# Who prepares the expert weights of a fused attention, MLP and mixture-of-experts kernel: VectorE with GpSimd, or VectorE alone

## The chip, the core and the metric

The kernel runs on one core of a Trainium2 chip. The metric is the device time of one execution in microseconds (us). The engines of the core run side by side, each through its own list of instructions in order: TensorE (PE in the profile, with PEld for its weight loads), VectorE (DVE), ScalarE (ACT), GpSimd (POOL) and SyncE (SP), which here issues the transfers between the memory on the chip and HBM. They wait for each other through semaphores.

## What is computed

The reference does three things in a row, in float32: attention over keys and values that are averaged in groups of eight, a two-layer MLP, and a mixture of eight experts. Only the last one matters here:

```python
def _moe2_ref(x, w_gate, w1, w2):          # x 2304 x 512, w1 8 x 512 x 1024, w2 8 x 1024 x 512
    logits = x @ w_gate
    ...                                     # exp and eight Sinkhorn steps give P, 2304 x 8
    for e in range(E):
        h = np.maximum(x @ w1[e], 0.0)
        ye = h @ w2[e]
        out += P[:, e:e + 1] * ye
```

## The kernel before, in words

**Numbers in two parts.** A product of two float32 matrices is made from three products of a faster format (fp32r): each matrix is split into a high part, which ScalarE rounds off, and a low part, which is the difference between the matrix and its high part. `halves` (line 964) does this: `activate` for the high part (`whi`, `vhi`, `gh`), then one `tensor_tensor` subtraction for the low part (`wlo`, `vlo`, `gl`), recorded at line 557 inside the helper `tt`.

**Seven products in the place of eight.** Each matrix is cut in four blocks, and sums and differences of the blocks (Strassen's scheme in Winograd's form, products P1 to P7) are multiplied.

**Units and steps.** The experts' weights come in 16 units, u = 0 to 15, each of 512 of the 1024 hidden columns of an expert. The tokens come in three pairs of blocks, taken in the order 1, 0, 2. So there are 48 steps (lines 1595 and 1630); a unit's weights serve three steps running. In a step the first layer (`first_layer`, line 1158, TensorE at line 1178, banks `px`, `py`, `pv`) of one step is interleaved with the second layer (`strassen_layer`, line 1555, TensorE at line 1565, banks `pc`, `qc`) of the step before it.

**The weights of a unit.** `w1_pieces` (line 1358) and `w2_pieces` (line 1394) load a unit's raw blocks (`raw`) and then make seven pieces each. Each function has four `combine` steps, which add or subtract two raw blocks into one of them (128 x 512, `raw<-raw` or `raw<-raw,raw` in the profile), and seven `cut` steps, which split a block (`whi` and `wlo`, or `vhi` and `vlo`). That is 22 `tensor_tensor` instructions of 128 x 512 a unit. The buffers for the pieces hold just one unit (W1 and W2 are 14 tiles, line 454), so a piece of the next unit can be written only when the last step of the present unit has read its own.

**Who waits for VectorE and ScalarE in a step.** In the first layer, `py<-px` (line 1184) is ScalarE's copy of one bank into another before TensorE goes on in it, and `pv<-py,s` (line 1189) is VectorE's sum of a bank and a copy, after which TensorE may use the bank `py` again. `c`, `spare`, `sf`, `gh`, `gl` make the next layer's operands, and `acc` gathers the results (line 1550).

**The order is planned.** No engine's order is written by hand: `Graph` (line 153) holds every step as a node with its engine and an estimated time, gives each a due time from its successors back (`latest`, line 208; a node that may run on two engines is counted with the longer of its two times), and then lists the nodes in simulated time (`schedule`, line 273): on each engine it takes, among the nodes that could start within a fraction of a microsecond of the earliest, the one that is due first. Nodes with `port=True` and GpSimd's nodes are not put side by side in the plan. Where a node may run on VectorE or GpSimd, the planner chooses:

```python
ALONE = [True]

def VG(n):
    return V(n) if ALONE[0] else {"engine": ("V", "G"), "us": (two(n), pool(n)), "port": True}
```

The `combine` and `cut` steps of the weights take their engine from `VG(FU)` (lines 1378, 1414 and, through `halves`, 968), with FU = 512. Before, `ALONE[0]` is set in one place only, at line 1235, to whether the task there is one of the first four; when the steps of the experts are recorded it is False.

Of the kernel before, what the change touches and what calls it, by code (L numbers as in the profile page):

```python
# [438 lines left out]
ALONE = [True]  # L439
# [9 lines left out]
def fused_kernel(ctx: ExitStack, tc: tile.TileContext, qT, kT, kS, vS, v0, k1, v1, wa1, wb1, wa2, wb2, wg, out):  # L449
# [908 lines left out]
    def w1_pieces(u):  # L1358

        src, w = [], {}  # L1360
        for i in range(2):
            src.append(buf(k_raw, [P, 2, FU], F32, "raw"))
        for i, t in enumerate(src):
            load(lambda t=t: t.tile, lambda i=i: wa2[u, :, i], P * 2 * FU * 4,
                 writes=[(t, 0), (t, 1)] + [(src[1], "room")] * (i == 0))

        def a(i, j):
            t = src[i - 1]
            return (t, j - 1), lambda: t[:, j - 1, :]

        def cut(name, what):
            parts = piece_tiles((k_w1, k_w1), ("whi", "wlo"), [P, FU])
            halves(FU, what[1], what[0], lambda k: parts[k].tile, parts)
            for h in range(2):
                w[name, h] = parts, lambda h=h: [t[:, h * HD:(h + 1) * HD] for t in parts]

        def combine(out, x, y, op):
            tt(VG(FU), out[1], x[1], y[1], op, [b[0] for b in (x, y) if b[0] != out[0]], [out[0]])

        a11, a12, a21, a22 = a(1, 1), a(1, 2), a(2, 1), a(2, 2)  # L1380
        cut("P1", a11)
        cut("P4", a22)
        combine(a22, a21, a22, ALU.add)
        cut("P5", a22)
        combine(a21, a11, a21, ALU.subtract)
        combine(a22, a22, a11, ALU.subtract)
        cut("P6", a22)
        cut("P2", a12)
        cut("P7", a21)
        combine(a12, a12, a22, ALU.subtract)  # L1390
        cut("P3", a12)
        return w

    def w2_pieces(u, goal=FAR):

        src, w = [], {}
        for h in range(2):
            t = buf(k_raw, [P, 2, DM], F32, "raw2")
            src.append(t)
        for h, t in enumerate(src):  # L1400
            load(lambda t=t: t.tile, lambda h=h: wb2[u, :, h], P * 2 * DM * 4,
                 writes=[(t, 0), (t, 1)] + [(src[1], "room")] * (h == 0))

        def b(h, d):
            t = src[h - 1]
            return (t, d - 1), lambda: t[:, :, (d - 1) * HD:d * HD]

        def cut(name, what):
            w[name] = parts = piece_tiles((k_w2, k_w2), ("vhi", "vlo"), [P, FU])
            halves(FU, what[1], what[0], lambda k: parts[k].tile.rearrange("p (g n) -> p g n", g=2), parts,  # L1410
                   goal=goal)

        def combine(out, x, y):
            tt(VG(FU), out[1], x[1], y[1], ALU.subtract, [q[0] for q in (x, y) if q[0] != out[0]], [out[0]])

        b11, b12, b21, b22 = b(1, 1), b(1, 2), b(2, 1), b(2, 2)
        cut("P1", b11)
        combine(b11, b12, b11)
        cut("P5", b11)
        combine(b12, b22, b12)  # L1420
        combine(b11, b22, b11)
        cut("P6", b11)
        cut("P2", b21)
        cut("P7", b12)
        cut("P3", b22)
        combine(b21, b21, b11)
        cut("P4", b21)
        return w
# [37 lines left out]
    def x_loaded(pair):  # L1466

        x = {}
        for name in ORDER:
            t = buf(k_x, [P, 2, 2, NB], F32R, "xc")  # L1470
            load(lambda t=t: t.tile.bitcast(F32), lambda name=name: xc[pair, ORDER.index(name)], P * 4 * NB * 4,
                 reads=[kept_x[pair, name]], writes=[t])
            x[name] = [t], lambda t=t: (t[:, 0], t[:, 1])
        return x
# [153 lines left out]
    boxes = [{} for _ in range(NTP)]  # L1628
    g.lap = False
    for n, (u, pair) in enumerate(steps):  # L1630
        if pair == steps[0][1]:
            w1, w2 = w1_pieces(u), w2_pieces(u, FAR if u else end - 40.0)
        pieces = {}
        first_layer(w1, ready if n == 0 else x_loaded(pair), strassen_result(pieces), goals1[n])
        own = {2: (b_x, b_y)} if n == len(steps) - 1 else None
        strassen_layer(pair, u, pieces, w2, boxes[pair], goals2[n], own)
# [60 lines left out]
```

## Time and profile before

| | us |
|---|---|
| median of 3 runs | 1916.88 |
| lowest and highest | 1916.5 and 1919.01 |
| the profiled execution's own time | 1917.53 |
| its span, from first to last instruction | 1915.8 |
| TensorE busy | 1891.6 |
| VectorE busy | 1511.9 |
| ScalarE busy | 1098.1 |
| GpSimd busy | 360.3 |

The span lies 1.73 us under the profiled execution's own time, and that execution lies 0.65 us over the median. Busy time adds the durations of an engine's instructions. TensorE's granted clock is at its upper level, 2.4 GHz, through the span. The experts' steps begin at about 500 us; a unit takes 87.9 us, and 16 of them reach to the end.

### The profile page before, as it was taken

To read this page: it belongs to the slowest core of one execution; us is meant where nothing else is said; L and a number is where in the kernel's file an instruction comes from. 1 tells how busy PE (TensorE), PEld (TensorE's weight loads), DVE (VectorE), ACT (ScalarE), POOL (GpSimd) and SP (SyncE) were. 2 spreads that over 40 slices of the span, in tenths; PEclk is the share of its full clock that TensorE was granted. 3 is DMA by queue.
4 is the path that set the end of the run, shared out by engine and by line. 5 is a ranking of instruction groups with operands and counts; after the bars stand their busy time and mean duration, and the time that the engine had idled before them with its cause. 6 is when DMAs were issued, how large, how long until landed. Compare 5 with 4: busy or idle time off the path is not lost.

```text
span 1915.8 us, 33914 instructions
## 1 busy us (share of the span) xinstructions
PE 1891.6 (99%) x13032; PEld 1850.2 (97%) x13032; DVE 1511.9 (79%) x2720; ACT 1098.1 (57%) x2372; POOL 360.3 (19%) x264
## 2 busy tenths in 40 slices
PE   9999999999999999999999999999999999999999
PEld 7799998899999999999999999999999999999999
DVE  7998856987687777777787787777777877878776
ACT  5875435675566665555556555565555555555653
POOL 0203332252112121212112021212121120212120
PEclk9999999999999999999999999999999999999999
DMA  8856662577665646546546455565465464655553
GB/s 265 245 197 234 237 164 80 196 265 256 232 234 223 239 175 242 223 176 234 217 174 264 168 234 226 191 238 214 179 240 210 181 264 157 245 215 195 234 203 127
DMA packets 104762, 406.76 MB, mean 212 GB/s; under 512 B 11160, under 2 KB 15896, under 8 KB 102552
## 3 DMA queue, kind: packets, MB, share of 16 engines
q1 hardware_dynamic: 102616, 400.01, 56.1%
q0 software_dynamic: 1984, 4.59, 1.4%
q8 instruction: 102, 1.67, 0.4%
q14 instruction: 60, 0.49, 0.1%
HBM read 363.40 MB, written 41.16 MB: 211 GB/s over the span
## 4 chain that ended last, share of the span: by engine, by line
PE 85%; DVE 9%; issue 2%; DMA 2%; ACT 2%; SPq 0%; POOL 0%; POOLq 0%; DVEq 0%; ACTq 0%
PE pc L1565 18%; PE py L1178 15%; PE qc L1565 15%; PE pv L1178 10%; PE px L1178 10%; PE po L989 3%; PE po L991 3%; PE po L990 3%; PE ph L989 2%; PE ph L991 2%; PE ph L990 2%; DVE sf L557 2%; DVE raw L557 1%; DVE gl L557 1%; DVE vlo L557 1%
## 5 line engine op out<-in xcount | busy, mean ns | idle before, releaser
L1565 PE MATMUL pc<-vhi,gl 128*128 128x256 f32 x1152 | 318.2, 276 | 0.0
L1565 PE MATMUL pc<-vlo,gh 128*128 128x256 f32 x1152 | 318.0, 276 | 0.0
L1565 PE MATMUL pc<-vhi,gh 128*128 128x256 f32 x1152 | 318.0, 276 | 0.0
L1178 PE MATMUL py<-xc,whi 128*128 128x384 f32 x1152 | 297.1, 338 | 9.4 <-ACT py L540 5.1
L1565 PE MATMUL qc<-vhi,gh 128*128 128x256 f32 x864 | 238.7, 276 | 0.2 <-DVE qc L557 0.2
L1565 PE MATMUL qc<-vlo,gh 128*128 128x256 f32 x864 | 238.5, 276 | 0.0
L1565 PE MATMUL qc<-vhi,gl 128*128 128x256 f32 x864 | 238.5, 276 | 0.0
L540 ACT ACTIVATE gh<-sf 128x384 fp32r<-128x384 f32 x384 | 195.4, 524 | 63.6 <-DVE sf L557 59.2
L557 DVE TENSOR_TENSOR gl<-sf,gh 128x384 fp32r<-128x384 f32 x384 | 204.0, 561 | 31.8 <-ACT gh L540 31.6
L557 POOL TENSOR_TENSOR raw<-raw 128x512 f32<-128x512 f32 x47 | 62.3, 1326 | 874.3 <-DVE wlo L557 492.2
L1565 PEld LDWEIGHTS pc<-vhi,gl 128*128 128x128 f32 x1152 | 216.2, 188 | 0.1
L1565 PEld LDWEIGHTS pc<-vhi,gh 128*128 128x128 f32 x1152 | 216.2, 188 | 0.1
L1565 PEld LDWEIGHTS pc<-vlo,gh 128*128 128x128 f32 x1152 | 216.2, 188 | 0.0
L1178 PEld LDWEIGHTS py<-xc,whi 128*128 128x128 f32 x1152 | 199.0, 188 | 17.7 <-ACT py L540 10.3
L1178 PE MATMUL px<-xc,whi 128*128 128x384 f32 x768 | 196.4, 336 | 0.2 <-DMA xc<-xc 0.2
L1178 PE MATMUL pv<-xc,whi 128*128 128x384 f32 x768 | 195.9, 336 | 0.0
L1178 PE MATMUL py<-xc,wlo 128*128 128x384 f32 x576 | 192.6, 334 | 0.0
L1565 PEld LDWEIGHTS qc<-vhi,gh 128*128 128x128 f32 x864 | 162.2, 188 | 0.5 <-DVE qc L557 0.5
L1565 PEld LDWEIGHTS qc<-vhi,gl 128*128 128x128 f32 x864 | 162.2, 188 | 0.0
L1565 PEld LDWEIGHTS qc<-vlo,gh 128*128 128x128 f32 x864 | 162.0, 187 | 0.0
L1178 PEld LDWEIGHTS pv<-xc,whi 128*128 128x128 f32 x768 | 132.1, 188 | 0.0
L540 ACT ACTIVATE qc<-pc 128x256 f32<-128x256 f32 x144 | 53.1, 369 | 136.7 <-PE pc L1565 136.6
(245 smaller groups left out, 4671.4 us busy)
## 6 DMA issues: line engine op xcount, KB each, us to landing
xc<-xc SPq DMA_DIRECT2D x357, 768.0 KB, 6.8
wc<-wac SPq DMA_DIRECT2D x112, 256.0 KB, 4.7
raw<-wb SPq DMA_DIRECT2D x32, 512.0 KB, 7.7
raw<-wa SPq DMA_DIRECT2D x32, 512.0 KB, 3.8
raw<-wa SPq DMA_DIRECT2D x8, 1024.0 KB, 7.3
raw<-wb SPq DMA_DIRECT2D x8, 1024.0 KB, 6.0
wac<-m SPq DMA_DIRECT2D x12, 512.0 KB, 6.3
wac<-cw SPq DMA_DIRECT2D x12, 512.0 KB, 3.1
```

The costliest lines, as they stand in the source:

```text
L540: lambda: nc.scalar.activation(out=out(), in_=in_(), func=func, **{k: v() if callable(v) else v for k, v in more.items()}),
L557: (nc.gpsimd if e == "G" else nc.vector).tensor_tensor(out=out(), in0=in0(), in1=in1(), op=op)
L989: nc.tensor.matmul(out=ps, lhsT=lh, rhs=rh, start=(i == 0), stop=False)
L990: nc.tensor.matmul(out=ps, lhsT=lh, rhs=rl, start=False, stop=False)
L991: nc.tensor.matmul(out=ps, lhsT=ll, rhs=rh, start=False, stop=(i == total - 1))
L1178: nc.tensor.matmul(out=ps(), lhsT=l[:, k], rhs=r[:, c, :], start=(start and c + n == 0), stop=(c + n == 3), skip_group_check=True)
L1565: nc.tensor.matmul(out=ps, lhsT=l[:, r], rhs=m[:, k], start=(start and h + n == 0), stop=(h + n == 3), skip_group_check=True)
```

## The change

One line is added. As the steps of the experts are recorded, `ALONE[0]` is set to whether the unit is not the first, so from the second unit (u = 1) on `VG` gives the planner VectorE alone for the 22 `combine` and `cut` instructions of a unit. Unit 0, and all that is recorded before the experts, keep the choice between the two engines.

```diff
     boxes = [{} for _ in range(NTP)]
     g.lap = False
     for n, (u, pair) in enumerate(steps):
+        ALONE[0] = u > 0
         if pair == steps[0][1]:
             w1, w2 = w1_pieces(u), w2_pieces(u, FAR if u else end - 40.0)
         pieces = {}
```

## Rows read from the trace of the kernel before

**Rows 1.** Busy time by stretches; columns in the first line, x counts instructions.
```profile
core 0: us, PE busy (x) PEld busy (x) DVE busy (x) ACT busy (x) POOL busy (x), PEclk, DMA share, GB/s
0.00:500.00 500.00, 489.76 (x2909) 459.26 (x2910) 404.31 (x668) 292.49 (x584) 126.37 (x93) 1.00 0.64 211
600.00:690.00 90.00, 90.00 (x653) 89.82 (x653) 68.85 (x127) 63.43 (x137) 16.47 (x12) 1.00 0.57 218
690.00:1880.00 1190.00, 1180.23 (x8516) 1172.21 (x8515) 933.19 (x1690) 665.22 (x1490) 201.05 (x149) 1.00 0.56 213
```

**Rows 2.** TensorE's waits, 700 to 1900 us: total, times, longest.
```profile
PE py L1178 <- ACT py L540: 5.1, 13, 0.4
PE py L1178 <- DVE pv L557: 4.4, 14, 0.6
```

**Rows 3.** Timeline of TensorE: start, duration, instruction, idle time before it and releaser.
```profile
1036.32 0.51 PE L1178 MATMUL py<-xc,whi 128*128 128x384 f32 x2
...
1048.94 0.62 PE L1178 MATMUL py<-xc,whi 128*128 128x384 f32 x2 [0.39 <-ACT py L540]
...
1054.31 0.45 PE L1178 MATMUL py<-xc,whi 128*128 128x384 f32 x1 [0.29 <-DVE pv L557]
```

**Rows 4.** Timeline of ScalarE around the first of the two waits.
```profile
1035.47 0.47 ACT L540 ACTIVATE py<-px 128x384 f32<-128x384 f32 x1 [2.45 <-PE px L1178]
...
1047.87 0.63 ACT L540 ACTIVATE vhi<-raw 128x512 fp32r<-128x512 f32 x1 [1.01 <-DVE raw L557]
1048.41 0.47 ACT L540 ACTIVATE py<-px 128x384 f32<-128x384 f32 x1
```

**Rows 5.** Timeline of VectorE in the same unit.
```profile
1042.36 0.43 DVE L557 TENSOR_TENSOR pc<-qc,t 128x256 f32<-128x256 f32 x1 [0.46 <-PE pc L1565]
...
1046.15 1.69 DVE L557 TENSOR_TENSOR raw<-raw,raw 128x512 f32<-128x512 f32 x1
...
1049.48 2.13 DVE L557 TENSOR_TENSOR gl<-spare,gh 128x384 fp32r<-128x384 f32 x2
1051.53 1.64 DVE L557 TENSOR_TENSOR sf<-spare 128x384 f32<-128x384 f32 x1
...
1053.70 0.55 DVE L557 TENSOR_TENSOR pv<-py,s 128x384 f32<-128x384 f32 x1
...
1054.63 1.01 DVE L557 TENSOR_TENSOR gl<-sf,gh 128x384 fp32r<-128x384 f32 x2
...
1097.15 1.10 DVE L557 TENSOR_TENSOR wlo<-raw,whi 128x512 fp32r<-128x512 f32 x1
...
1106.21 1.43 DVE L557 TENSOR_TENSOR wlo<-raw,whi 128x512 fp32r<-128x512 f32 x1
```

**Rows 6.** Timeline of GpSimd in the same unit.
```profile
1042.33 1.29 POOL L557 TENSOR_TENSOR raw<-raw,raw 128x512 f32<-128x512 f32 x1
...
1045.99 1.30 POOL L557 TENSOR_TENSOR vlo<-raw,vhi 128x512 fp32r<-128x512 f32 x1 [1.10 <-ACT vhi L540]
1049.51 1.68 POOL L557 TENSOR_TENSOR vlo<-raw,vhi 128x512 fp32r<-128x512 f32 x1 [2.21 <-ACT vhi L540]
1051.16 1.60 POOL L557 TENSOR_TENSOR raw<-raw,raw 128x512 f32<-128x512 f32 x1
```

**Rows 7.** VectorE's instructions that read `raw`: shortest/median/longest ns, first and last start.
```profile
L557 DVE TENSOR_TENSOR wlo<-raw,whi x79: 679/694/1441, 472.1 to 1810.1; 128x512 fp32r<-128x512 f32 x79
...
L557 DVE TENSOR_TENSOR raw<-raw,raw x17: 678/1685/1691, 451.9 to 1838.0; 128x512 f32<-128x512 f32 x17
```

**Rows 8.** Busy time in one unit and in three parts of it; columns as in rows 1.
```profile
1046.00:1134.00 88.00, 87.32 (x633) 86.75 (x632) 68.99 (x126) 49.16 (x111) 14.86 (x12) 1.00 0.55 212
1038.00:1045.00 7.00, 7.00 (x53) 7.00 (x53) 3.56 (x8) 5.25 (x13) 3.86 (x3) 1.00 0.98 370
1045.00:1061.00 16.00, 15.32 (x108) 14.80 (x107) 15.54 (x25) 9.65 (x23) 4.55 (x3) 1.00 0.48 190
1096.00:1110.00 14.00, 14.00 (x99) 13.95 (x98) 11.57 (x20) 10.99 (x25) 5.09 (x4) 1.00 0.95 383
```

## The prediction

> **What bounds the kernel now.** I read the busy time by stretches first. From 690 to 1880 us TensorE is busy 1180.23 of 1190 us, at a granted clock of 1.00; its idle time there is 9.77 us [rows 1]. So whatever the change does to VectorE, it can give back about 10 us in the experts' steps, 0.5%, and no more: TensorE's own work is not touched. The other idle time, 10.24 us, lies before 500 us [rows 1], where nothing changes engine.
>
> The list of TensorE's waits comes second. Nearly all of the idle time is in two waits, 5.1 us in 13 and 4.4 us in 14, both in front of matmuls into `py` [rows 2]. They come once each in a unit, at the same place: in the unit shown 0.39 us at 1048.94 and 0.29 us at 1054.31 [rows 3]. All other hand-overs of a unit, some hundred of them, cost TensorE nothing.
>
> The timelines of the other engines around these two places come third, and there GpSimd can be seen. At 1046.15 VectorE's `raw<-raw,raw` takes 1.69 us [rows 5], while its shortest is 678 ns [rows 7]; GpSimd's `vlo` had started at 1045.99 and ended at 1047.29 [rows 6]. At 1049.48 two `gl<-spare,gh` take 2.13 us where two of the same size take 1.01 at 1054.63, and `sf<-spare` takes 1.64 [rows 5]; GpSimd's `vlo` and `raw` run from 1049.51 to 1052.76, and they are stretched too, to 1.68 and 1.60 from 1.30 [rows 6]. An instruction of VectorE that takes one input from a PSUM bank isn't stretched: `pc<-qc,t` takes 0.43 us at 1042.36 with GpSimd's `raw` beside it from 1042.33 to 1043.62 [rows 5, 6]. So what the two engines do on two SBUF inputs excludes each other: one waits until the other is through.
>
> The first wait of TensorE follows from the first collision. The stretched `raw` ends at 1047.84; ScalarE's `vhi` has waited 1.01 us for it, starts at 1047.87, and `py<-px` stands behind `vhi` in ScalarE's queue, from 1048.41 to 1048.88 [rows 4, 5]; TensorE goes on at 1048.94 [rows 3]. The second wait follows from the second collision: `pv<-py,s` stands in VectorE's queue behind the stretched instructions, ends at 1054.25 [rows 5], and TensorE goes on at 1054.31 [rows 3].
>
> **The change part by part.** Removed: GpSimd's share of the weights, 149 instructions with 201.05 us between 690 and 1880 us, eleven in a unit (the twelve of the unit's row hold one that belongs to the next) [rows 1, 8]. Added: eleven instructions of 0.69 us on VectorE (median of `wlo` 694 ns [rows 7]), 7.6 us a unit. Removed with GpSimd: the stretches, 1.69 - 0.68 = 1.01, 2.13 - 1.01 = 1.12 and 1.64 - 0.55 = 1.09 in the first part of the unit, and 1.10 - 0.69 = 0.41 and 1.43 - 0.69 = 0.74 in the later one [rows 5, 7], together 4.4 us. VectorE's busy time in a unit goes from 68.99 [rows 8] to 68.99 + 7.6 - 4.4 = 72.2 us of 88, from 78% to 82%. On the average there is room; what counts is the three parts in which GpSimd works.
>
> From 1038 to 1045 three instructions move, 2.1 us; VectorE is busy 3.56 of 7 us there [rows 8], so they fit. From 1045 to 1061 three more move, 2.1 us, and the 3.2 us of stretch go: VectorE gains 1.1 us in the part in which it is busy 15.54 of 16 us [rows 8]. From 1096 to 1110 four move, 2.8 us, against 1.15 us of stretch; VectorE is busy 11.57 of 14 us [rows 8] and goes to 13.2. That is the tightest place of the changed kernel, and TensorE waits for nothing there now (14.00 of 14).
>
> The first wait, by the present order: with `vlo` on VectorE (0.69) ahead of `raw` (0.69), the two take from 1046.0 to 1047.4, `vhi` on ScalarE ends at about 1048.0 and `py<-px` 0.47 later, at 1048.5; TensorE was free at 1048.94 - 0.39 = 1048.55 [rows 3, 4]. So the wait goes, with a margin of about nothing in this order and of 0.7 us with `raw` first. The second wait: `pv<-py,s` moves forward by those 1.1 us, against a wait of 0.29 [rows 3]. Both go: 5.1 + 4.4 = 9.5 us [rows 2].
>
> What comes back is not shown in this trace. VectorE alone makes the planner list everything anew, and an added instruction of 0.69 us can stand in front of one that TensorE waits for. From below: nothing comes back. That this can be is shown from 600 to 690 us, where GpSimd works as much (16.47 us) and TensorE is busy 90.00 of 90 us [rows 1]: an order without a wait exists for the same work, with collisions. From above: all of the 9.5 us come back, or more (the rivals). I take 1.0 us, since the quiet stretch is the same work in the same steps and so the nearest row. The stretch before 500 us is planned by the same list, and due times of the later weights shift by the difference of the two engines' times; I cost that at nothing, with 1 us either way as a tenth of the 10.24 us that TensorE idles there [rows 1].
>
> Sum: the profiled execution took 1917.53 us, so 1917.53 - 9.5 + 1.0 = 1909.0. It lay 0.65 above the median of the runs shown, 1916.88, so a median of 1908.4.
>
> **The rivals.** No change: the waits only change their cause. With `vlo` first, the margin at the first place is 0.05 us, and VectorE's queue keeps a new 0.69 us instruction in front of `pv<-py,s` in each unit. Then TensorE idles about as long as now, and the time is 1916.9, or anything above 1913.05 (0.2% is about what a measurement of this kernel can tell from no change). For it speaks that the planner knows nothing of a hand-over's real slack; against it, that the present order has eleven such VectorE instructions in a unit already, and none without a collision costs TensorE a wait.
>
> Slower: VectorE's queue becomes the bound of the hand-overs. In an undisturbed step `py<-px` ends at 1035.94 and TensorE needs it at 1036.32 [rows 3, 4], a slack of 0.38 us, of which 0.06 go for the signal (1048.88 to 1048.94). An added piece of 0.69 us that starts just before what such a hand-over needs costs 0.69 - 0.32 = 0.37 us. In the part from 1096 to 1110, with 13.2 of 14 us, all four moved ones can do so: 1.5 us a unit, in 14 units 20.7 us, less 9.5, gives 1916.9 + 11 = 1928. It decides from the point where it is three a unit (1.1 us against 0.69 gained). Against it: most hand-overs have more slack than this one, and the planner can place a piece late. Here a rule of the Trainium skill speaks against the change: Perfetto Trace Analysis, section Optimizing Scalar/DVE Operations, says that with VectorE saturated it may pay to offload work to other engines, GpSimd among them, though it adds that sharing a port can void it. By its first half the time would be this rival's; the rows bear out the second half where VectorE is fullest.
>
> The change does not do what it says: `ALONE[0]` is read when a node is recorded, the line stands ahead of both calls, and nothing sets it back; I give that no chance.
>
> **How the numbers follow.** Forecast (both waits gone, little back) 0.70; no change 0.17; slower 0.13. The likeliest time is 1908.4. Its own range: 9.5 us and 1 us early on give 1906.4 at the low end, and 3 us back with 1 us early 1912 at the high end. The range that should hold 8 in 10 takes in most of the no-change case: 1906 to 1918. Faster by over 0.2% 0.70, within 0.2% 0.17, slower 0.13.
>
> **What would show it.** Right: no GpSimd instruction after about 600 us; VectorE's `raw` and `wlo` all near 0.69 us and none over 1 us; TensorE's two waits gone from the list, and its busy time over 99.8% from 690 to 1880 us; VectorE's busy time in a unit near 72 us. Wrong: new waits in front of `py` or `pc` with VectorE's pieces or an instruction behind them as their releaser, first of all in the part that answers to 1096 to 1110 us; or a longer stretch before 500 us, which would be the planner's doing.

## The result and the profile after

The changed kernel takes 1899.8 us (median of 5 runs, 1898.25 to 1900.2) against 1916.88 of the kernel before (1916.29 to 1919.01): a ratio of 0.9907, 95% interval 0.9892 to 0.9921. It is 17 us faster, where 8.5 us were forecast, and lies below the range of 1906 to 1918. The span of the profiled execution is 1898.0 us, 17.8 us less than before.

Busy time by stretches of the kernel after, the columns as in [rows 1]:

```profile
0.00:500.00 500.00, 489.92 (x2911) 459.62 (x2912) 405.11 (x669) 292.98 (x584) 127.43 (x93) 1.00 0.65 211
600.00:690.00 90.00, 90.00 (x656) 90.00 (x655) 70.26 (x137) 62.38 (x135) 0.00 (x0) 1.00 0.57 216
690.00:1862.00 1172.00, 1172.00 (x8520) 1172.00 (x8519) 955.66 (x1842) 660.45 (x1492) 0.00 (x0) 1.00 0.57 217
```

The last line answers to the last of [rows 1]. It holds nearly the same number of matmuls (8520 and 8516) in a stretch that is 18.0 us shorter. TensorE waits for nothing in it: 1172.00 of 1172.00 us, in the matmuls (PE) and in the weight loads (PEld). Before, the matmuls were busy 1180.23 of 1190 us, 9.77 idle, and the weight loads 1172.21, 17.79 idle [rows 1]. The gain of the span, 17.8 us, has the size of the idle time of the weight loads, not of that of the matmuls. Before 500 us hardly anything has moved: the weight loads are busy 459.62 us, and were 459.26 [rows 1].

The durations of the instructions that read `raw`, in the kernel after (shortest, median, longest in ns), answer to [rows 7]:

```profile
L557 DVE TENSOR_TENSOR vlo<-raw,vhi x111: 681/684/800, 449.1 to 1837.5; 128x512 fp32r<-128x512 f32 x111
L557 DVE TENSOR_TENSOR wlo<-raw,whi x111: 681/685/694, 471.6 to 1798.6; 128x512 fp32r<-128x512 f32 x111
L557 DVE TENSOR_TENSOR raw<-raw x78: 680/682/693, 450.4 to 1817.9; 128x512 f32<-128x512 f32 x78
L557 DVE TENSOR_TENSOR raw<-raw,raw x47: 681/684/686, 451.5 to 1834.4; 128x512 f32<-128x512 f32 x47
```

From the second unit's weights on nothing in these rows is stretched: `raw<-raw,raw`, whose median was 1685 ns, takes 684, and the longest `wlo` went from 1441 to 694 ns. (The one `vlo` of 800 ns lies before 600 us, where GpSimd still works on unit 0.) A unit of the kernel after, 86.68 us long (87.94 before, from one unit's loads of `raw` to the next), reads:

```profile
1028.60:1115.28 86.68, 86.68 (x632) 86.68 (x632) 70.65 (x137) 48.69 (x110) 0.00 (x0) 1.00 0.57 216
```

VectorE is busy 70.65 us with eleven instructions more than in [rows 8], where it was busy 68.99.

### The profile page after: what moved, and what is told of

Same layout as the page of the kernel before. It is cut to its first block, busy times and chain, and to the rows that moved or that the text cites. A ratio compares the mean times of both kernels' runs of the same rounds, so it can differ in the third digit from the quotient of the medians.

```text
span 1898.0 us, 33781 instructions
## 1 busy us (share of the span) xinstructions
PE 1883.5 (99%) x13040; PEld 1850.3 (97%) x13040; DVE 1538.1 (81%) x2888; ACT 1091.3 (57%) x2371; POOL 135.6 (7%) x97
## 4 chain that ended last, share of the span: by engine, by line
PE 93%; DVE 4%; ACT 1%; DMA 1%; issue 0%; SPq 0%; DVEq 0%; ACTq 0%
PE pc L1565 21%; PE py L1178 17%; PE qc L1565 16%; PE pv L1178 11%; PE px L1178 11%; PE po L989 3%; PE po L991 3%; PE po L990 3%; PE ph L989 2%; PE ph L991 2%; PE ph L990 2%; PE px L897 0%; PE psc L776 0%; DMA xc<-xc 0%; PE ptr L883 0%
## 5 line engine op out<-in xcount | busy, mean ns | idle before, releaser
L540 ACT ACTIVATE gh<-sf 128x384 fp32r<-128x384 f32 x384 | 190.0, 522 | 29.5 <-DVE sf L557 26.9
L1178 PEld LDWEIGHTS px<-xc,whi 128*128 128x128 f32 x768 | 128.3, 188 | 0.6 <-issue 0.6
```

The costliest lines, as they stand in the source:

```text
L540: lambda: nc.scalar.activation(out=out(), in_=in_(), func=func, **{k: v() if callable(v) else v for k, v in more.items()}),
L1178: nc.tensor.matmul(out=ps(), lhsT=l[:, k], rhs=r[:, c, :], start=(start and c + n == 0), stop=(c + n == 3), skip_group_check=True)
```

## The experiments

The theory after the result: GpSimd's instructions on the weights of the second layer lock out VectorE at two places of a unit; each place makes TensorE wait; and a wait costs TensorE more than the idle time that its matmul row shows. The rivals: the planner's new listing brings the gain; VectorE's load matters, wherever the work is; the matmul row's idle time is the whole price, and the rest of the gain has another source.

**The old plan, executed by VectorE alone.** The planner still hands pieces to GpSimd and lists everything as before; only as the instruction is issued does VectorE take the place of GpSimd.

```diff
@@ tt
+        turned = TURNED[0]
+
         def run(e=how["engine"]):
-            (nc.gpsimd if e == "G" else nc.vector).tensor_tensor(out=out(), in0=in0(), in1=in1(), op=op)
+            (nc.gpsimd if e == "G" and not turned else nc.vector).tensor_tensor(out=out(), in0=in0(), in1=in1(), op=op)
...
+            TURNED[0] = u > 0
             w1, w2 = w1_pieces(u), w2_pieces(u, FAR if u else end - 40.0)
+            TURNED[0] = False
```

> The plan of the kernel before is kept, node by node (the planner still believes that GpSimd does its share), but from the second unit on VectorE executes GpSimd's pieces too, at the place in its queue that the plan's order of starts gives. Theory (collisions): without GpSimd the stretches go and with them the two waits, though nothing is planned anew: 1899 to 1903 us. Rival (the new listing brings the gain): the hand-overs stay where they are, and the pieces stand in front of them as GpSimd's lock did: 1912 to 1918.

Measured: 1899.41 us (4 runs), ratio 0.9908 (0.9888 to 0.9928). The instructions of TensorE, ScalarE and SyncE stand in the same order as in the kernel before; in the kernel after, those of these three engines and of VectorE stand otherwise. So the whole gain comes without a new plan. The rival of the new listing falls. Busy time from 690 to 1860 us of this run:

```profile
690.00:1860.00 1170.00, 1170.00 (x8490) 1167.92 (x8489) 953.98 (x1835) 666.02 (x1486) 0.00 (x0) 1.00 0.57 217
```

The place of the first wait, in VectorE's and ScalarE's timelines of this run:

```profile
1040.99 0.69 DVE L560 TENSOR_TENSOR raw<-raw,raw 128x512 f32<-128x512 f32 x1
1041.60 0.74 DVE L1553 SCALAR_TENSOR_TENSOR acc<-qc,pr,acc 128x512 f32<-128x512 f32 x1
1042.26 0.68 DVE L560 TENSOR_TENSOR vlo<-raw,vhi 128x512 fp32r<-128x512 f32 x1
```

```profile
1042.25 0.47 ACT L541 ACTIVATE py<-px 128x384 f32<-128x384 f32 x1
```

The `vlo` that GpSimd made at 1045.99 in the kernel before [rows 6] now starts at 1042.26, behind `raw` and not ahead of it; that it is this one is read from the order of the neighbours. `py<-px` ends at 1042.72, and TensorE goes on without a wait in its list.

The weight loads idle 2.08 us in this run, most of it once a unit for 0.11 us, in the part that answers to 1096 to 1110 us. There `qc<-qc,t` stands behind a piece that was GpSimd's, and ends at 1097.84. VectorE, then the weight loads:

```profile
1096.82 0.68 DVE L560 TENSOR_TENSOR raw<-raw 128x512 f32<-128x512 f32 x1
1097.42 0.42 DVE L560 TENSOR_TENSOR qc<-qc,t 128x256 f32<-128x256 f32 x1
```

```profile
1097.60 0.19 PEld L1181 LDWEIGHTS py<-xc,wlo 128*128 128x128 f32 x1
1097.90 0.19 PEld L1568 LDWEIGHTS qc<-vhi,gh 128*128 128x128 f32 x1
```

**One half of the weights at a time.** In the first kernel the line sets `ALONE[0]` for `w2_pieces` only, in the second for `w1_pieces` only.

```diff
-            w1, w2 = w1_pieces(u), w2_pieces(u, FAR if u else end - 40.0)
+            w1 = w1_pieces(u)
+            ALONE[0] = u > 0
+            w2 = w2_pieces(u, FAR if u else end - 40.0)
+            ALONE[0] = False
```

```diff
-            w1, w2 = w1_pieces(u), w2_pieces(u, FAR if u else end - 40.0)
+            ALONE[0] = u > 0
+            w1 = w1_pieces(u)
+            ALONE[0] = False
+            w2 = w2_pieces(u, FAR if u else end - 40.0)
```

> From the second unit on, only the pieces of the second layer's weights (w2_pieces) are made by VectorE alone; those of the first layer's (w1_pieces) keep the choice. Theory (collisions): both of TensorE's waits of a unit come from collisions with GpSimd's work on w2, so both go, though GpSimd still works on w1: 1899 to 1903 us, TensorE's weight loads idle under 3 us from 690 us on. Rival (the new listing by the planner brings the gain, wherever the work moves): something between the two kernels, 1904 to 1913.

> The other half: only the pieces of the first layer's weights are made by VectorE alone; those of the second layer's keep the choice. Theory (collisions): the instructions that collide ahead of the two waits work on w2 and stay, so the waits stay: 1914 to 1918 us. Rival (VectorE's load or the new listing decides): 1904 to 1911.

Measured: 1899.23 us with w2 alone (4 runs; ratio 0.9906, 0.9885 to 0.9927) and 1915.55 with w1 alone (10 runs; 0.9995, 0.9983 to 1.0006). All of the gain lies in w2, none that can be told in w1. The first kernel, where GpSimd still works on w1, has collisions that cost TensorE nothing. The durations of VectorE's `wlo` and GpSimd's pieces in it:

```profile
L557 DVE TENSOR_TENSOR wlo<-raw,whi x79: 678/693/1520, 470.2 to 1791.1; 128x512 fp32r<-128x512 f32 x79
...
L557 POOL TENSOR_TENSOR raw<-raw x33: 1287/1297/1681, 471.0 to 1788.3; 128x512 f32<-128x512 f32 x33
L557 POOL TENSOR_TENSOR wlo<-raw,whi x33: 1287/1295/1664, 477.5 to 1790.8; 128x512 fp32r<-128x512 f32 x33
```

VectorE's `wlo` is still stretched to as much as 1520 ns, and TensorE's matmuls are busy 1169.86 of 1170 us from 690 to 1860 all the same, its weight loads 1169.49: no hand-over without slack stands behind these collisions.

```profile
690.00:1860.00 1170.00, 1169.86 (x8502) 1169.49 (x8502) 940.61 (x1786) 662.74 (x1486) 66.15 (x52) 1.00 0.57 216
```

In the second kernel TensorE's waits, in matmuls and in weight loads, stay (total, times, longest; those of before in matmuls are in [rows 2]):

```profile
PE py L1178 <- ACT py L540: 5.5, 14, 0.4
PE py L1178 <- DVE pv L557: 4.0, 14, 0.3
```

```profile
PEld py L1178 <- ACT py L540: 9.9, 14, 0.7
PEld py L1178 <- DVE pv L557: 6.8, 14, 0.5
```

**A part of the units.**

```diff
-        ALONE[0] = u > 0
+        ALONE[0] = u > 7
```

> VectorE alone from the ninth unit's weights on (u > 7 in place of u > 0). Theory: the loss is 1.26 us in each unit from the third unit's weights on (period 87.94 us before, 86.68 after), so the weights of units 2 to 7 keep six of the fourteen losses: 1899.8 + 6 x 1.26 = 1907.4, 1906 to 1909. Rival (a part of the gain comes once, from the planning of the whole): off that line, under 1904 or over 1911.

Measured: 1907.03 us (5 runs, 1906.73 to 1909.09; ratio 0.995, 0.9934 to 0.9966), against 1907.4 by six losses of 1.26 us. Its list of TensorE's waits has six for `pv` and five for `py<-px`, where that of before has 14 and 13 [rows 2]. The gain is a sum over units.

```profile
PE py L1178 <- DVE pv L557: 2.0, 6, 0.6
PE py L1178 <- ACT py L540: 2.0, 5, 0.4
```

**The price of a wait.** In the changed kernel ScalarE's copy `py<-px` is done three or four times in the first half of each step, so that TensorE waits at a place and for a time of our choosing.

```diff
+                    def copy(y=y, ps=ps, times=copies if h == 0 else 1):
+                        for _ in range(times):
+                            nc.scalar.activation(out=y[:, :NB], in_=ps(), func=AF.Copy)
+
+                    add("A", actp(NB), copy, [bank], [y])
-                    activate(NB, lambda y=y: y[:, :NB], ps, reads=[bank], writes=[y], from_psum=True)
```

> The changed kernel, in which ScalarE does the copy py<-px of the first half of each of the 48 steps three times in place of once (the same values), which the planner doesn't know of. It is to price a wait of TensorE. The three copies end about 1.29 us after px, and py, which has 0.89 us from px to its start, begins about 0.47 us late where px, pv and py follow each other (32 to 48 of the 48 places). Theory (a wait costs more than the idle time in TensorE's matmul row, since that row counts the tail of a pipelined matmul as busy and the restart shows the weight load): each costs 0.47 + 0.12 = 0.59 us, 1919 to 1928 us in all, the weight loads' idle time (PEld) grows by as much as the span, and the matmuls' idle time (PE) by about half of it. Rival (the matmul row's idle time is the price): the span grows by that idle time alone, 0.31 us each, 1910 to 1915.

> As the kernel with three copies, with four. Theory and rival differ in the price of the first wait and agree on that of its lengthening: one more copy (0.39 us) adds 0.39 us at each place that waits already, 12 to 19 us over three copies. In the rows of one execution: span less that of the changed kernel equals the growth of PEld's idle time (theory), or of PE's (rival).

Measured: 1936.92 us with three copies (4 runs; ratio 1.0094, 1.0071 to 1.0116) and 1963.02 with four (4 runs; 1.0227, 1.0202 to 1.0252). Both lie above what theory and rival had expected. A further copy takes 0.51 us and not the 0.39 that was counted: three take 1.49 us and four 2.00.

```profile
1027.73 1.49 ACT L1186 ACTIVATE py<-px 128x384 f32<-128x384 f32 x3
```

```profile
1067.98 2.00 ACT L1186 ACTIVATE py<-px 128x384 f32<-128x384 f32 x4
```

The question was the price of each wait that this makes. The waits of the two kernels from 500 us on, total, times, longest, first with three copies, for the matmuls and then for the weight loads:

```profile
PE py L1178 <- ACT py L1186: 24.3, 46, 0.5
```

```profile
PEld py L1178 <- ACT py L1186: 39.4, 46, 1.2
```

and with four copies:

```profile
PE py L1178 <- ACT py L1186: 47.9, 47, 1.0
```

```profile
PEld py L1178 <- ACT py L1186: 63.2, 47, 1.7
```

| | span, us | more than the kernel after | these waits in the matmuls | these waits in the weight loads |
|---|---|---|---|---|
| three copies | 1936.8 | 38.8 | 24.3 | 39.4 |
| four copies | 1961.7 | 63.7 | 47.9 | 63.2 |

The span grows by the weight loads' waits, to within 0.6 us, and by 14.5 and 15.8 us more than the matmuls' waits: 0.32 and 0.34 us for each of the 46 and 47 waits, at a mean wait of 0.53 and of 1.02 us in the matmul row. The rival that the matmul row gives the price falls. The timeline of TensorE in the kernel with three copies shows where those 0.3 us lie:

```profile
1028.06 0.51 PE L1178 MATMUL pv<-xc,whi 128*128 128x384 f32 x2
1028.40 0.34 PE L1178 MATMUL pv<-xc,wlo 128*128 128x384 f32 x1
1029.28 0.62 PE L1178 MATMUL py<-xc,whi 128*128 128x384 f32 x2 [0.54 <-ACT py L1186]
1029.73 0.34 PE L1178 MATMUL py<-xc,wlo 128*128 128x384 f32 x1
```

Undisturbed, as in the kernel after, one matmul of this size follows the other by 0.18 us and a pair by 0.34:

```profile
1043.32 0.33 PE L1178 MATMUL pv<-xc,wlo 128*128 128x384 f32 x1
1043.50 0.51 PE L1178 MATMUL py<-xc,whi 128*128 128x384 f32 x2
1043.84 0.33 PE L1178 MATMUL py<-xc,wlo 128*128 128x384 f32 x1
```

So `py` was due at 1028.40 + 0.18 = 1028.58 and began 0.70 us later, though the row says 0.54: the last matmul before the wait is drawn with its full 0.34 us, of which 0.16 would have lain under the next one. And the first pair after the wait takes 1029.73 - 1029.28 = 0.45 us in place of 0.34. Together 0.16 + 0.11 = 0.27 us that no idle time of the matmul row shows.

**GpSimd beside a VectorE that does all the work.** In the changed kernel GpSimd works on raw blocks that nobody reads again, in five places of a unit that the planner knows nothing of (`behind` is set for P7 and P3 of w1 and for P7, P3 and P4 of w2, from the second unit on).

```diff
+        if behind:
+            low = node.run
+
+            def run():
+                low()
+                nc.gpsimd.tensor_tensor(out=src(), in0=src(), in1=out(0).bitcast(F32), op=ALU.subtract)
+
+            node.run = run
```

> The changed kernel, and GpSimd does idle work beside it that the planner doesn't know of: behind five of the fourteen splits of a unit it subtracts the high part once more from a raw block that nobody reads again (five instructions of 128 x 512 a unit, in place). VectorE does all of its own work. Theory (collisions): VectorE's instructions with two SBUF inputs are stretched again, by up to about 1 us each, TensorE waits at some of these places, and the time rises by some 0.3 to 1.2 us a unit: 1904 to 1920. Rival (the moved work or the new plan is what matters, not GpSimd's presence): 1898 to 1901.

Measured: 1910.65 us (10 runs; ratio to before 0.9965, 0.9954 to 0.9977), 10.9 us more than the kernel after. VectorE does the same instructions at the same planned places as in that kernel, so GpSimd's presence alone costs this. Its mechanism is the one read before, at another hand-over. GpSimd, VectorE and TensorE in one unit:

```profile
1053.97 3.09 POOL L975 TENSOR_TENSOR raw<-raw,vhi 128x512 f32<-128x512 f32 x2 [29.84 <-ACT c L540]
```

```profile
1054.26 3.68 DVE L557 TENSOR_TENSOR gl<-sf,gh 128x384 fp32r<-128x384 f32 x3
1057.87 0.42 DVE L557 TENSOR_TENSOR pc<-qc,t 128x256 f32<-128x256 f32 x1
```

```profile
1058.34 0.39 PE L1574 MATMUL qc<-vhi,gh 128*128 128x256 f32 x1 [0.47 <-DVE pc L557]
```

Two of GpSimd's instructions run from 1053.97 to 1057.06. Three `gl<-sf,gh`, each 0.55 us where nothing collides, take 3.68 beside them; `pc<-qc,t` stands behind them and ends at 1058.29; TensorE goes on at 1058.34. The weight loads idle 0.79 us at this place, where the matmul row shows 0.47, fifteen times in the kernel (12.1 and 7.3 us). The time rose by 10.9 us and the span by 10.4, between the two sums and nearer to that of the weight loads. No other GpSimd instruction of a unit has a wait of TensorE behind it in the list from 500 us on.

```profile
PE qc L1574 <- DVE pc L557: 7.3, 15, 0.7
```

```profile
PEld qc L1574 <- DVE pc L557: 12.1, 15, 1.1
```

**VectorE alone from the start.** Line 1235 is left out, so that `ALONE[0]` stays true in the attention, the MLP and the first unit too.

```diff
-        ALONE[0] = task < ONE
```

> VectorE alone for all that asks for a choice by VG, from the start of the kernel (the first expert unit, the MLP's weights and the attention too); only the steps of 128 x 768 keep the choice. Theory: before 500 us TensorE's weight loads idle some 40 us, mostly for other reasons than GpSimd, and VectorE is busier there (0.92 from 100 to 200 us); a gain of up to 3 us over the changed kernel where collisions are hidden in it, a loss of up to 4 where VectorE is full: 1896 to 1904.

Measured: 1902.69 us (4 runs, 1901.7 to 1903.23; ratio to before 0.9921, 0.9904 to 0.9937). It is no better than the kernel after, and its runs all lie above those of it (1898.25 to 1900.2), though the intervals of the two ratios overlap (0.9904 to 0.9937 and 0.9892 to 0.9921). The weight loads idle as long before 500 us as in the kernel after (40.28 and 40.38 us of 500) and are no more idle from 690 us on; so taking GpSimd's work away there gains TensorE nothing. Where the 2.7 us of its span lie isn't settled: 1.6 of them are idle time of the weight loads between 500 and 690 us.

None of the runs beats the kernel after by more than they scatter.

## Why the prediction was wrong

**The mechanism was right.** That GpSimd and VectorE exclude each other on two SBUF inputs; that the stretched `raw<-raw,raw` and `gl`, `sf` cause the two waits through ScalarE's and VectorE's queues; that the waits sit in the weights of the second layer; that VectorE alone has room for all pieces: each was borne out, by the old plan executed by VectorE, by the two halves, and by GpSimd working beside. The margin of 0.05 us at the first place, for `vlo` ahead of `raw`, was not put to the test. The prediction took this for the present order, but in the old plan executed by VectorE `raw` comes first (1040.99 and 1042.26), and in the kernel after both stand elsewhere.

**The step that failed is the first one: the bound.** "It can give back about 10 us in the experts' steps, 0.5%, and no more" takes the idle time of the matmul row, 9.77 us, for what TensorE loses. What it loses is close to the idle time of the weight loads: 1190 - 1172.21 = 17.79 us in the very same line of [rows 1], one column on. The span fell by 17.8. The weight loads' waits of the kernel before, 700 to 1900 us, are the same 13 and 14 as in [rows 2]:

```profile
PEld py L1178 <- ACT py L540: 9.2, 13, 0.7
PEld py L1178 <- DVE pv L557: 7.1, 14, 0.8
```

They come to 16.3 us, where the matmul row has 9.5: 0.32 us more for each of the first and 0.19 for each of the second. In the unit shown the matmul row has 0.39 and 0.29 us [rows 3], 0.68 together, and a unit became 87.94 - 86.68 = 1.26 us shorter, so 0.58 us stayed out of sight of that row. The waits made with more copies have 0.32 to 0.34 us each that it doesn't show.

The same mistake sits in "TensorE was free at 1048.55", against which the margin at the first place was set:

```profile
1048.21 0.34 PE L1178 MATMUL pv<-xc,wlo 128*128 128x384 f32 x1
```

The matmul is drawn to 1048.55, but at the undisturbed distance of 0.18 us the next one was due at 1048.39.

What TensorE's profile rows mean was to be had before: matmuls overlap in the trace (two of 128 x 384, 0.33 us each, take 0.51 at 1036.32 [rows 3]), so the matmul row counts the tail of the last one before a wait as busy. The Trainium skill, Perfetto Trace Analysis, section Identifying the Most-Contended Engine, says that matmul busy time is no good measure of how near TensorE is to its roofline, and that its headroom is judged by the weight loads' busy share, beside the share of peak arithmetic. The trace agrees: total weight-load time is 1850.2 us before and 1850.3 after, and the spans, 1915.8 and 1898.0, differ by the rest.

**The other steps.** The term that comes back, put at 1.0 us, was nothing: 1172.00 of 1172.00. The quiet stretch from 600 to 690 us, from which it was bounded below, was the right guide. VectorE's busy time in a unit, worked out as 72.2 us, is 70.65: the stretches that went were about 68.99 + 7.6 - 70.65 = 5.9 us and not 4.4. The stretch before 500 us, costed at nothing with 1 us either way, changed by 0.4 us of weight-load time. With 17.8 in the place of 9.5 and nothing given back, the same sum gives 1916.88 - 17.8 = 1899.1; measured 1899.8. The range was too narrow at its low end because it was made of the failed bound: I had written that TensorE cannot give more, and let the range go no further. Its high-end case was added up wrongly as well: 3 us back and 1 us lost early on give 1916.9 - 9.5 + 3 + 1 = 1911.4 and not 1912, which changes nothing here.

**The rivals.** No change (0.17) and slower (0.13) both needed VectorE's added instructions to get in the way of a hand-over. In the kernel after none did. In the old plan one did, by 0.11 us a unit in the weight loads, in the part from 1096 to 1110 us that I had named as the tightest: the mechanism of the slower rival exists, at 0.11 us against the 1.5 us a unit that it was given. That part is where w1 is made; moving that half alone made no difference that can be told (1915.55). The Trainium skill's advice to offload work from a full VectorE to GpSimd, in Perfetto Trace Analysis, section Optimizing Scalar/DVE Operations, is one to weigh by its own caveat on the shared port: here VectorE was 97% busy in the part that mattered [rows 8], and part of that was waiting for GpSimd.

## What to carry to other kernels

Where TensorE is the bound, take what can be gained from the idle time of the weight loads, or from the distance between starts of matmuls against that of an undisturbed stretch; the matmul row's idle time missed 0.2 to 0.34 us of a wait in these runs, which is as much as a short wait itself. Before handing VectorE's work to GpSimd, look for what VectorE does on two SBUF inputs in the same microseconds and for the hand-over queued behind it: in these runs a collision cost nothing where there was slack behind it, and where there was too little a part of itself (with GpSimd beside, some 2 us of stretch cost TensorE 10.4 / 15 = 0.7 us a unit). A change of engine can be told from the new plan that it brings by keeping the plan and changing only the engine that executes.

## What was not expected of the hardware

A wait of TensorE has a part that the matmul row doesn't show and that hardly grows with its length: 0.32 us a wait at 0.53 us of shown idle time (24.3 over 46) and 0.34 at 1.02 (47.9 over 47). It differs by place, from 0.19 us for the waits for `pv` to 0.32 for those for `py<-px` in the kernel before. A copy by ScalarE of 128 x 384 out of a PSUM bank into the same tile as the copy before it follows after 0.51 us (three in 1.49, four in 2.00, one in 0.47); I had counted 0.39. GpSimd is held up by VectorE as VectorE by GpSimd: its 128 x 512 took 1.28 us alone and 3.09 for two beside VectorE's `gl`.
